# A fused attention and gated MLP kernel: w_in's DRAM writes queued behind batch 0's last store, w_out's blocks combined in batch 1's first half, seven products in its second

## The chip, the cores and the metric

The kernel runs on one core of a Trainium2 chip. The core has a matmul engine (TensorE, PE in the profile; its weight loads are shown as PEld), a vector engine (VectorE, DVE), a scalar engine (ScalarE, ACT), a general engine (GpSimd, POOL) and a queueing engine (SyncE, SP). Each works through its own instructions in order and meets the others at semaphores. On-chip data lies in SBUF, matmul results in the eight banks of PSUM, everything else in DRAM; 16 DMA engines move data between DRAM and SBUF. Nearly all DMAs of this kernel are issued by SP.

The metric is device time in microseconds of one execution, lower is better.

## The reference

The computation is a packed attention followed by a gated MLP. There are 8 batches with 8 heads, 576 positions and head dimension 64; 32 packed queries `p` per head first attend to the keys, then the 576 queries attend to the 32 results:

```python
p_packed = sm_attn(p, k, v)              # softmax(p k^T / 8) v, per batch and head
out = sm_attn(q, p_packed, p_packed)
x = out.transpose(0, 2, 1, 3).reshape(4608, 512)
h = x @ w_in                             # 512 x 2048
g = h * np.clip(h + 3.0, 0.0, 6.0) / 6.0
return g @ w_out                         # 2048 x 512
```

All inputs are float32 to the reference; `w_in` and `w_out` come as 64-bit words that the kernel narrows to float32 itself (lines 173 to 199).

## The kernel before

**The two products.** The kernel never forms `x`. For each batch it makes `m` = packed result times `w_in` (256 x 2048: 8 heads with 32 packed rows each; `u_m`, line 518, in four column chunks n) and multiplies the second softmax's weights by it. The 2048 columns of the hidden layer are walked in 16 blocks `f` of 128. For each block, `first_product` (line 912) makes the hidden values of up to 320 positions, `gate_into` (928) applies ACT's relu and DVE's min-and-multiply, `split` (935) makes a high part (ACT copy, rounded) and a low part (POOL subtraction), and the second product multiplies them by the rows of `w_out` that belong to `f`. Every exact product is three matmuls of rounded parts: high x high, high x low, low x high. So the first product of a block is 2 groups of 3 matmuls, and the second is 3 matmuls for each 128 positions, 512 columns wide.

**Halves of a batch.** A batch's 576 positions are done in two halves c = 0 and 1. One of them is "wide": it also computes 64 edge positions, kept in `bnd` and multiplied with those of a neighbouring batch, 128 at a time (`edge_parts`, `edge_product`). Second products wait in the list `pend` and are issued one or two blocks late, so that the matmul engine has other work while the gate is made.

**The seven products.** `moe_pairs` (1071) takes the blocks f = 0 to 7 as four pairs. A pair is a 2 x 2 matrix of 128-wide blocks times the 2 x 2 blocks of `w_out` (B11, B12 in the rows of block 2i; B21, B22 in those of 2i + 1; each 128 x 256). Instead of eight block products it makes seven, from sums of the blocks: S1 to S4 of the gated values (four additions on DVE, lines 1171 to 1174) and T1 to T4 of `w_out`. Each product is 3 matmuls, 256 columns wide. They are gathered in four PSUM banks A to D, whose numbers stand in `roles`. The blocks 8 to 15 are done singly. Batches 2 to 7 use `moe_pairs`; batch 1 uses `moe` (997), which does all 16 blocks singly; batch 0 has code of its own, `first_moe` (1202).

**combine.** The T blocks are made once, during batch 1, by `combine(i)` (1040), i = 0 to 3. T1, T2 and T4 go to new tiles that take the room of w_in's chunks 1 to 3 in SBUF (`wt`, tags `w_in1` to `w_in3`); T3 overwrites B12 inside `w_out`. Each `combine` adds high and low part of the two rows of blocks on POOL, makes the differences on DVE, then the parts on ACT and DVE. It is a generator: `fill` (1360), called ahead of each block f, moves it on by three steps in the second half from f = 2i + 4.

**w_in.** Later batches need w_in again, but only chunk 0's room (`w_in0`) stays for it. `keep_w_in(n)` (1334) writes the narrowed chunk n, 1 MB, to the DRAM tile `w_kept`; `fetch_w_in(n)` (1337) reads it back for the `u_m` of the next batch. Before the change `fill` calls `keep_w_in` in the first four blocks of batch 1.

**What sets the order.** Batch 0 follows `PLAN` (31 to 51), an order written by hand for all five engines; `lo` and `li` in it are loads of weights, `o0` to `o3` batch 0's output stores (`stored`, 1248). From batch 1 on, the order of the instructions on each engine is worked out ahead, when the program is built, from dependences and priorities; `issue_after(x)` keeps what is traced inside it behind x on x's engine. Nothing keeps `keep_w_in` behind batch 0's instructions, so its DMAs stand among batch 0's loads on SP. `fill` also brings in the next batch's attention: `inputs` (loads and transposes) from step 0, `packed` (the first softmax and its product) from step 6, `ahead` (`u_s2`, the second softmax) from step 19 of batch 1's 32 steps (`STAGES`, 23).

**PSUM.** `moe` takes its banks in turn from four (`next_acc`): three in the wide half, then two. The scores of the next batch's attention take a bank that is free; once `roles` is set, `u_s2` makes its scores in two rounds instead of one (478).

Of the kernel before, what the change touches and what calls it, by code (L numbers as in the profile page):

```python
# [10 lines left out]
F32 = mybir.dt.float32  # L11
# [5 lines left out]
ALU = mybir.AluOpType  # L17
# [7 lines left out]

LATE = (3, 2, 1, 2, 1)
PAIRS = 4

# [41 lines left out]
def packed_attention_moe(  # L72
# [17 lines left out]
    nc = tc.nc  # L90
    B, H, S, D = q.shape
    NPK = p.shape[2]
    DM, DF = w_in.shape
# [32 lines left out]
    def wo_at(part, f):  # L126
        return wo[f >= EARLY][part][:, f - EARLY * (f >= EARLY)]
# [912 lines left out]
    def combine(i):  # L1040

        if i == 0:
            for n in (2, 3, 1):
                for k in range(4):
                    blocks[len(blocks)] = n, k
            tiles = {
                n: wr.tile([P, 4, 2, H2], F32R, name=f"wt{n}", tag=f"w_in{n}") for n in (1, 2, 3)
            }
            for k in range(3 * PAIRS):
                n, at = blocks.pop(k)  # L1050
                blocks[k // 3, ("T1", "T2", "T4")[k % 3]] = [tiles[n][:, at, x] for x in range(2)]
        x = [xp.tile([P, 6 * P], F32, name="wx", tag="raw") for _ in range(2)]
        for k in range(2):
            hi, lo = (wo_at(part, 2 * i + k).bitcast(F32) for part in ("hi", "lo"))
            nc.gpsimd.tensor_tensor(out=x[k][:, :DM], in0=hi, in1=lo, op=ALU.add)
            yield
        b11, b12, t1 = (x[0][:, k * H2:(k + 1) * H2] for k in range(3))
        b21, b22, t2 = (x[1][:, k * H2:(k + 1) * H2] for k in range(3))
        nc.vector.tensor_sub(out=t1, in0=b12, in1=b11)
        nc.vector.tensor_sub(out=t2, in0=b22, in1=t1)  # L1060
        yield
        nc.vector.tensor_sub(out=b12, in0=b12, in1=b22)
        nc.vector.tensor_sub(out=b21, in0=b21, in1=t2)
        yield
        for name, made in (("T1", t1), ("T2", t2), ("T4", b21), ("T3", b12)):
            hi, lo = block(i, name)
            nc.scalar.copy(out=hi, in_=made)
            nc.vector.tensor_sub(out=lo, in0=made, in1=hi.bitcast(F32))
            yield

    def moe_pairs(b, c, fill):

# [129 lines left out]
    def first_moe(chains):  # L1202
# [45 lines left out]
        def stored(i):  # L1248

            osb = gp.tile([P, DM], F32, name="osb")  # L1250
            nc.scalar.activation(out=osb, in_=accs[i], func=AF.Copy, scale=1.0 / 6.0)
            yield
            rows = out[:4 * P].rearrange("(r c) m -> c r m", c=4)[2 * (i % 2) + i // 2]
            nc.sync.dma_start(out=rows, in_=osb)
            yield

        for f in range(NF):
# [91 lines left out]
    for b in range(1, B):  # L1349
# [10 lines left out]
        def fill(c, f):  # L1360
            s = c * NF + f
            with behind_gates():
                if b == 1:
                    for _ in range(LATE[s] if s < len(LATE) else 0):
                        next(late, None)
                    if s < NCH:
                        keep_w_in(s)
                    for i in range(PAIRS):
                        if c and f >= 2 * i + 4:
                            for _ in range(3):  # L1370
                                next(turned[i], None)
                else:
                    if s > 0:
                        next(late, None)
# [8 lines left out]
                        next(chain, None)  # L1383

        for c in range(2):
            if b == 1:
                moe(b, (c,), lambda f, c=c: fill(c, f))
            else:
                moe_pairs(b, c, lambda f, c=c: fill(c, f))
        if b == 1:  # L1390
            rest(*turned)
            roles.extend((acc_count[0] + i) % 4 for i in (2, 3, 0, 1))
    with tc.manual_schedule(engines={mybir.EngineType.PE}):
        second(0)

# [28 lines left out]
```

## Time and profile before

| | us |
|---|---|
| median of 3 runs | 727.02 |
| lowest, highest | 725.9, 727.23 |
| the profiled execution | 728.73 |
| its span on the core | 727.0 |

The profile is of one execution. Its span runs from the first to the last instruction on the core; the profiled execution's own time also has what lies around it. A second table shows how the span is used in 40 equal slices (18.2 us each): each digit is the busy share in tenths, PEclk is the clock granted to the matmul engine in tenths of full speed, DMA the mean share of the 16 DMA engines.

```profile
PE   6598899999989999999999999999999999999997
DVE  2896678541898568674596567685396856964252
PEclk9799999999999999999999999999999999999999
DMA  9999973435117162543524445272342723320000
```

The first six slices are batch 0, in most of which the DMA engines are at nine tenths or more. Batch 1's first half begins in slice 7 (counted from one), its second half about slice 10, batch 2 in slice 13. Other parts of the profile used below are the timelines of single engines (start, duration, engine, line, operation, output and inputs, and in brackets the idle time before it and what ended it), groups of instructions by line (busy us, mean ns of one, idle time before) and the chain of waits (start, duration, engine, output, line). The matmul engine's durations overlap, since its matmuls are pipelined; the chain's pieces do not.

### The profile page before, as it was taken

Reading aid. Unit: us, or ns where it says so; the run is one execution under the profiler, and the core shown is the slowest. Engines: PE = TensorE matmul, PEld = TensorE weight load, DVE = VectorE, ACT = ScalarE, POOL = GpSimd, SP = SyncE. Lnnn points to the kernel's source line nnn. Section 1 sums busy time; section 2 is a strip of 40 time slices with the busy share of each in tenths; the row PEclk is TensorE's granted clock in tenths of the full one; section 3 lists DMA queues with packets and bytes.
Section 4 is the critical chain, followed back from the end, with each engine's and each line's share of the span. In section 5 each row is a group of like instructions: output and inputs, shape, how many; then the busy total and the mean of one; then the engine's idle time right before and its main releaser. Section 6 shows DMA issues by size and latency. Waiting matters only on the chain.

```text
span 727.0 us, 15138 instructions
## 1 busy us (share of the span) xinstructions
PE 696.1 (96%) x5636; PEld 584.1 (80%) x5636; DVE 466.7 (64%) x1021; ACT 404.1 (56%) x884; POOL 354.2 (49%) x503
## 2 busy tenths in 40 slices
PE   6598899999989999999999999999999999999997
PEld 4476777788758887898887988798887988789896
DVE  2896678541898568674596567685396856964252
ACT  5797776553556555565355555555365554654362
POOL 2564440434455455474263535566353535557462
PEclk9799999999999999999999999999999999999999
DMA  9999973435117162543524445272342723320000
GB/s 280 294 259 265 262 226 85 85 61 125 73 58 175 30 154 79 167 78 62 139 71 156 79 96 149 74 175 50 91 119 81 166 54 98 116 87 1 27 19 29
DMA packets 195066, 85.41 MB, mean 117 GB/s; under 512 B 172976, under 2 KB 184752, under 8 KB 191408
## 3 DMA queue, kind: packets, MB, share of 16 engines
q1 hardware_dynamic: 194448, 84.24, 44.4%
q8 instruction: 44, 0.72, 0.4%
q14 instruction: 30, 0.25, 0.1%
q10 hardware_dynamic: 544, 0.20, 0.1%
HBM read 70.78 MB, written 13.63 MB: 116 GB/s over the span
## 4 chain that ended last, share of the span: by engine, by line
PE 79%; DVE 9%; DMA 5%; ACT 2%; SPq 2%; issue 2%; POOL 1%; ACTq 0%; POOLq 0%; DVEq 0%
PE acc L952 46%; PE ps_hh L919 23%; PE ps L340 5%; PE ps_h L597 2%; PE ps L460 1%; DMA room<-in_q_dram 1%; DMA w_again<-w_kept 1%; DVE t L931 1%; DMA out_dram<-osb_j 1%; PE ps L430 1%; SPq L284 1%; DMA raw_out<-in_moe_w_out_dram 1%; DMA raw_in<-in_moe_w_in_dram 1%; DVE z L505 1%; DMA p_nat<-in_p_dram 1%
## 5 line engine op out<-in xcount | busy, mean ns | idle before, releaser
L952 PE MATMUL acc<-wo_hi,g 128*128 128x512 f32 x512 | 182.6, 399 | 2.9 <-POOL g L937 2.9
L931 DVE SCALAR_TENSOR_TENSOR t<-t,ps_hh 128x320 f32<-128x320 f32 (+1 forms) x176 | 79.1, 449 | 121.3 <-ACT t L930 114.5
L937 POOL TENSOR_TENSOR g<-t,g 128x256 fp32r<-128x256 f32 x128 | 101.5, 794 | 86.2 <-ACT g L936 69.2
L919 PE MATMUL ps_hh<-a_hi,m_hi 128*128 128x320 f32 (+1 forms) x448 | 136.0, 304 | 1.9 <-DVE t L931 1.8
L930 ACT ACTIVATE t<-ps_hh,three 128x320 f32<-128x320 f32 (+1 forms) x176 | 88.0, 500 | 83.5 <-PE ps_hh L919 75.4
L919 PE MATMUL ps_hh<-a_hi,m_lo 128*128 128x320 f32 (+1 forms) x448 | 133.1, 297 | 0.0
L919 PE MATMUL ps_hh<-a_lo,m_hi 128*128 128x320 f32 (+1 forms) x448 | 132.8, 297 | 0.0
L952 PEld LDWEIGHTS acc<-wo_hi,g 128*128 128x128 f32 x512 | 94.8, 188 | 30.4 <-POOL g L937 6.5
L919 PEld LDWEIGHTS ps_hh<-a_hi,m_hi 128*128 128x128 f32 x448 | 84.7, 189 | 20.8 <-DVE t L931 5.6
L952 PE MATMUL acc<-wo_lo,g 128*128 128x512 f32 x256 | 100.9, 394 | 0.0
L919 PEld LDWEIGHTS ps_hh<-a_lo,m_hi 128*128 128x128 f32 x448 | 84.8, 189 | 6.0 <-issue 1.4
L937 POOL TENSOR_TENSOR ga<-tb,ga 128x256 fp32r<-128x256 f32 x96 | 59.9, 625 | 57.8 <-ACT ga L936 52.0
L919 PEld LDWEIGHTS ps_hh<-a_hi,m_lo 128*128 128x128 f32 x448 | 84.8, 189 | 3.9 <-issue 3.4
L936 ACT CAST g<-t 128x256 fp32r<-128x256 f32 x128 | 51.8, 405 | 49.8 <-DVE t L931 48.8
L937 POOL TENSOR_TENSOR gl<-t,gh 128x512 fp32r<-128x512 f32 x48 | 64.1, 1335 | 18.6 <-DMA out_dram<-osb_j 6.3
L948 POOL COPY bnd<-t 128x64 f32<-128x64 f32 x88 | 23.6, 269 | 94.8 <-DVE t L931 92.3
L545 DVE STREAM_TRANSPOSE tr<-nat 128x576 f32<-128x576 f32 x56 | 42.3, 766 | 25.1 <-DMA nat<-in_q_dram 14.3
L952 PE MATMUL acc<-wo_hi,gl 128*128 128x256 f32 (+1 forms) x160 | 52.5, 328 | 2.3 <-DVE gl L1230 1.3
L952 PE MATMUL acc<-wo_hi,gh 128*128 128x256 f32 (+1 forms) x160 | 54.0, 337 | 0.0
L952 PEld LDWEIGHTS acc<-wo_lo,g 128*128 128x128 f32 x256 | 48.3, 189 | 6.9 <-issue 0.8
L952 PE MATMUL acc<-wo_hi,ga 128*128 128x256 f32 x192 | 53.1, 283 | 0.0
L952 PE MATMUL acc<-wo_lo,gh 128*128 128x256 f32 (+1 forms) x160 | 52.1, 326 | 0.0
(213 smaller groups left out, 1503.7 us busy)
## 6 DMA issues: line engine op xcount, KB each, us to landing
w_again<-w_kept SPq DMA_DIRECT2D x24, 1024.0 KB, 4.9
out_dram<-osb SPq DMA_DIRECT2D x33, 256.0 KB, 2.5
nat<-in_k_dram SPq DMA_DIRECT2D x112, 72.0 KB, 2.8
nat<-in_q_dram SPq DMA_DIRECT2D x112, 72.0 KB, 2.6
raw_out<-in_moe_w_out_dram SPq DMA_DIRECT2D x10, 512.0 KB, 5.0
raw_in<-in_moe_w_in_dram SPq DMA_DIRECT2D x10, 512.0 KB, 5.8
w_kept<-w_in_sb SPq DMA_DIRECT2D x4, 1024.0 KB, 6.9
v_nat<-in_v_dram SPq DMA_DIRECT2D x28, 128.0 KB, 2.9
```

The source lines that it names most:

```text
L284: nc.sync.dma_start(out=t[r:r + 32], in_=src[b, 2 * a + h, :, 32 * c:32 * c + 32].rearrange("(t i) j -> i t j", i=32),)
L340: nc.tensor.matmul(pair[x][NPK * a:NPK * a + NPK, :n], rows[half, a], c, start=True, stop=True)
L430: nc.tensor.transpose(out=pair[x][:, c * P:(c + 1) * P], in_=e[x][:, c * P:(c + 1) * P], identity=ident)
L545: nc.vector.transpose(out=t, in_=state.pop(("nat", which, b, a)))
L597: nc.tensor.matmul(h[:, hf, :HS], mm[:, g, fs], aa[:, hf * HS:(hf + 1) * HS], start=(g == 0 and i == 0), stop=(g == NG - 1 and i == 2),)
L919: state["first"] = nc.tensor.matmul(h[:, :n], mm[:, g, fs], aa[:, t0:t0 + n], start=(g == 0 and i == 0), stop=(g == NG - 1 and i == 2),)
L930: state["relu"] = nc.scalar.activation(out=t[:, :n], in_=h, func=AF.Relu, bias=three)
L931: state["gate"] = nc.vector.scalar_tensor_tensor(out=t[:, :n], in0=t[:, :n], scalar=6.0, in1=h, op0=ALU.min, op1=ALU.mult)
L936: nc.scalar.copy(out=hi, in_=x)
L937: nc.gpsimd.tensor_sub(out=lo, in0=x, in1=hi.bitcast(F32))
L948: nc.gpsimd.tensor_copy(out=bnd[:, f, side * REM:side * REM + REM], in_=t[:, boff:boff + REM])
L952: nc.tensor.matmul(out, lhs[x], rhs[y], start=first and i == 0, stop=last and i == 2, skip_group_check=True)
```

## The change

Three things are changed. First, `stored` keeps the last store of batch 0 in `state["stored"]`, and all four `keep_w_in` are traced in step 0 of batch 1 behind that store on SP's queue. Second, `combine` is written anew: it works with two tiles of 256 columns, which take the room of `tb` (a tile of the pairs) instead of `raw`, adds high and low part of B12 and B22 only, and takes B11 and B21 part by part in additional DVE instructions; its steps are spread over steps 5 to 15 of batch 1, the first half, by the table `TURN` (step numbers of `combine(0)` to `combine(3)`). The T tiles fill chunk 1's room first. Third, batch 1's second half is done by `moe_pairs`, and `roles` is set ahead of it.

```diff
@@ -25,6 +25,7 @@
 
 LATE = (3, 2, 1, 2, 1)
 PAIRS = 4
+TURN = ((5, 5, 6, 6, 7, 7, 7), (7, 8, 8, 9, 9, 9, 10), (10, 10, 11, 11, 12, 12, 12), (13, 13, 13, 14, 14, 15, 15))
 
 
 
@@ -1040,7 +1041,7 @@
     def combine(i):
 
         if i == 0:
-            for n in (2, 3, 1):
+            for n in (1, 2, 3):
                 for k in range(4):
                     blocks[len(blocks)] = n, k
             tiles = {
@@ -1049,24 +1050,39 @@
             for k in range(3 * PAIRS):
                 n, at = blocks.pop(k)
                 blocks[k // 3, ("T1", "T2", "T4")[k % 3]] = [tiles[n][:, at, x] for x in range(2)]
-        x = [xp.tile([P, 6 * P], F32, name="wx", tag="raw") for _ in range(2)]
-        for k in range(2):
-            hi, lo = (wo_at(part, 2 * i + k).bitcast(F32) for part in ("hi", "lo"))
-            nc.gpsimd.tensor_tensor(out=x[k][:, :DM], in0=hi, in1=lo, op=ALU.add)
-            yield
-        b11, b12, t1 = (x[0][:, k * H2:(k + 1) * H2] for k in range(3))
-        b21, b22, t2 = (x[1][:, k * H2:(k + 1) * H2] for k in range(3))
-        nc.vector.tensor_sub(out=t1, in0=b12, in1=b11)
-        nc.vector.tensor_sub(out=t2, in0=b22, in1=t1)
-        yield
-        nc.vector.tensor_sub(out=b12, in0=b12, in1=b22)
-        nc.vector.tensor_sub(out=b21, in0=b21, in1=t2)
-        yield
-        for name, made in (("T1", t1), ("T2", t2), ("T4", b21), ("T3", b12)):
+        x, y = (xp.tile([P, W + P], F32, name="wx", tag="tb")[:, :H2] for _ in range(2))
+
+        def whole(dst, name):
+            hi, lo = (z.bitcast(F32) for z in block(i, name))
+            nc.gpsimd.tensor_tensor(out=dst, in0=hi, in1=lo, op=ALU.add)
+
+        def parted(name, made):
             hi, lo = block(i, name)
             nc.scalar.copy(out=hi, in_=made)
             nc.vector.tensor_sub(out=lo, in0=made, in1=hi.bitcast(F32))
-            yield
+
+        whole(x, "T3")
+        yield
+        whole(y, "B22")
+        yield
+        nc.vector.tensor_sub(out=y, in0=x, in1=y)
+        hi, lo = (z.bitcast(F32) for z in block(i, "B11"))
+        nc.vector.tensor_sub(out=x, in0=x, in1=hi)
+        nc.vector.tensor_sub(out=x, in0=x, in1=lo)
+        yield
+        parted("T1", x)
+        yield
+        nc.vector.tensor_sub(out=x, in0=hi, in1=y)
+        nc.vector.tensor_add(out=x, in0=x, in1=lo)
+        parted("T2", x)
+        yield
+        hi, lo = (z.bitcast(F32) for z in block(i, "B21"))
+        nc.vector.tensor_sub(out=x, in0=hi, in1=x)
+        nc.vector.tensor_add(out=x, in0=x, in1=lo)
+        parted("T4", x)
+        yield
+        parted("T3", y)
+        yield
 
     def moe_pairs(b, c, fill):
 
@@ -1251,7 +1267,7 @@
             nc.scalar.activation(out=osb, in_=accs[i], func=AF.Copy, scale=1.0 / 6.0)
             yield
             rows = out[:4 * P].rearrange("(r c) m -> c r m", c=4)[2 * (i % 2) + i // 2]
-            nc.sync.dma_start(out=rows, in_=osb)
+            state["stored"] = nc.sync.dma_start(out=rows, in_=osb)
             yield
 
         for f in range(NF):
@@ -1363,12 +1379,13 @@
                 if b == 1:
                     for _ in range(LATE[s] if s < len(LATE) else 0):
                         next(late, None)
-                    if s < NCH:
-                        keep_w_in(s)
+                    if s == 0:
+                        with tc.issue_after(state["stored"].ins):
+                            for n in range(NCH):
+                                keep_w_in(n)
                     for i in range(PAIRS):
-                        if c and f >= 2 * i + 4:
-                            for _ in range(3):
-                                next(turned[i], None)
+                        for _ in range(TURN[i].count(s)):
+                            next(turned[i], None)
                 else:
                     if s > 0:
                         next(late, None)
@@ -1383,13 +1400,12 @@
                         next(chain, None)
 
         for c in range(2):
-            if b == 1:
+            if (b, c) == (1, 0):
                 moe(b, (c,), lambda f, c=c: fill(c, f))
+                rest(*turned)
+                roles.extend((3, 0, 1, 2))
             else:
                 moe_pairs(b, c, lambda f, c=c: fill(c, f))
-        if b == 1:
-            rest(*turned)
-            roles.extend((acc_count[0] + i) % 4 for i in (2, 3, 0, 1))
     with tc.manual_schedule(engines={mybir.EngineType.PE}):
         second(0)
```

## The prediction

> **What bounds the kernel now.** First the page's busy shares, then the table by stretches.
>
> ```profile
> span 727.0 us, 15138 instructions
> PE 696.1 (96%) x5636; PEld 584.1 (80%) x5636; DVE 466.7 (64%) x1021; ACT 404.1 (56%) x884; POOL 354.2 (49%) x503
> ```
>
> PE is busy 96% of the span, so time is won only where PE stands, or where it has less to do. The starts of the first product's matmuls cut the span into halves of a batch. Batch 1's first half runs from 124.86 to 174.61, its second to 220.53; batch 3's second half, which already takes seven products, from 347.39 to 390.54. Columns: length, then busy time and instructions of PE, PEld, DVE, ACT, POOL; granted clock, DMA share, GB/s.
>
> ```profile
> 124.86:174.61 49.75, 49.75 (x378) 40.20 (x376) 20.25 (x46) 24.29 (x56) 20.75 (x40) 1.00 0.42 89
> 174.61:220.53 45.92, 41.71 (x278) 30.82 (x277) 36.21 (x72) 24.14 (x59) 24.73 (x24) 1.00 0.22 71
> 194.00:200.00 6.00, 5.15 (x28) 3.87 (x27) 6.00 (x14) 4.15 (x10) 3.79 (x4) 1.00 0.34 141
> 200.00:206.00 6.00, 4.43 (x23) 2.90 (x21) 6.00 (x11) 2.63 (x6) 3.04 (x4) 1.00 0.00 0
> 206.00:212.00 6.00, 5.88 (x44) 4.03 (x43) 6.00 (x13) 4.04 (x10) 3.02 (x4) 1.00 0.48 175
> 212.00:218.00 6.00, 4.33 (x22) 3.25 (x22) 5.05 (x9) 3.24 (x10) 4.22 (x4) 1.00 0.00 1
> 347.39:390.54 43.15, 42.64 (x406) 35.22 (x404) 30.44 (x64) 20.96 (x47) 18.29 (x23) 1.00 0.38 108
> 215.36 0.97 PE L952 MATMUL acc<-wo_hi,g 128*128 128x512 f32 x3 [1.60 <-POOL g L937]
> ```
>
> **Batch 1's second half is bound by DVE.** DVE is full from 194 to 212, and PE stands 0.85 + 1.57 + 0.12 + 1.67 = 4.2 us from 194 to 218. PE's timeline (last row) names POOL's low parts; POOL is not full there, but its inputs come through DVE's gate. This is where `combine` and batch 2's second softmax share DVE.
>
> **Batch 0 is bound by loads.** Rows of the timelines, in order of time; the bracket is the idle time before the row and what ended it.
>
> ```profile
> 41.04 0.39 SPq L1335 DMA_DIRECT2D w_kept<-w_in_sb  x1
> 52.59 0.55 SPq L1335 DMA_DIRECT2D w_kept<-w_in_sb  x1
> 53.23 7.56 SPq L284 DMA_DIRECT2D nat<-in_q_dram  x4
> 65.31 0.78 DVE L545 STREAM_TRANSPOSE tr<-nat 128x576 f32<-128x576 f32 x1 [3.12 <-DMA nat<-in_q_dram]
> 66.71 0.50 PE L952 MATMUL acc<-wo_hi,gl 128*128 128x512 f32 x1 [1.31 <-DVE gl L1230]
> 69.05 0.40 PE L597 MATMUL ps_h<-a_hi,m_hi 128*128 128x288 f32 x1 [0.45 <-DVE t L1223]
> 78.01 0.60 SPq L1335 DMA_DIRECT2D w_kept<-w_in_sb  x1
> 85.38 0.78 DVE L545 STREAM_TRANSPOSE tr<-nat 128x576 f32<-128x576 f32 x1 [2.54 <-DMA nat<-in_q_dram]
> 87.26 0.67 ACT L187 ACTIVATE raw_out<-raw_out 128x512 f32<-128x512 f32 x1 [2.66 <-DMA raw_out<-in_moe_w_out_dram]
> 89.39 0.40 PE L597 MATMUL ps_h<-a_hi,m_hi 128*128 128x288 f32 x1 [2.13 <-DVE t L1223]
> 86.00:92.00 6.00, 3.87 (x38) 2.98 (x41) 4.63 (x11) 4.49 (x8) 2.13 (x3) 0.90 1.00 280
> 92.00:98.00 6.00, 6.00 (x116) 4.25 (x106) 3.31 (x9) 4.61 (x8) 3.99 (x4) 0.82 0.82 281
> DMA to landing us min/median/max: 4.3/6.9/11.7
> ```
>
> Read it so: a 1 MB write of w_in goes out at 52.59; the queue's next four loads then take 7.56 us merely to issue; DVE stands 3.12 us for one of them, and PE follows (1.31 + 0.45). The same happens behind the write at 78.01: DVE 2.54, ACT 2.66, PE 2.13. Then the granted clock falls to 0.90 and 0.82 for two stretches of 6 us: 6 x 0.10 + 6 x 0.18 = 1.7 us of full clock. The last row gives the four writes' times to landing, 4.3 to 11.7 us.
>
> **Part 1: the writes leave batch 0.** Three of the four lie in the crowded stretch. What hangs on them is 1.31 + 0.45 + 2.13 = 3.9 us of standing and 1.7 us of clock, 5.6 together. The first write, at 41.04, goes too. All else is kept: the plan's order on PE, DVE, ACT, POOL and SP is fixed by hand, so the loads simply land earlier. I take 4.8: some 0.8 us for the next load that becomes the latest (from 86 to 92 DMA is 100% busy with loads alone). Bounds: 0, if the loads are late anyway, and 5.6; I stay near the top because both waits end directly behind a write.
>
> The Trainium skill (TensorE: Matmul & The Clock Gate, "What's actually happening") says the half-rate clock comes after at least one idle window of about 3.4 us. This trace shows the drop after 2.13 us of standing, so the trace decides; by the page the drop would have another cause and part 1 would be 1.7 us smaller.
>
> **Part 2: seven products in batch 1's second half.** Matmul pieces of the chain of waits, old form and batch 2's pair form; then DVE and POOL groups of this half (busy us, mean ns, idle before); the last row is line 505 in batch 3's second half.
>
> ```profile
> 177.61 2.80 PE acc L952 x12
> 228.03 1.44 PE acc L952 x12
> L1068 DVE TENSOR_TENSOR wt<-wx,wt 128x256 fp32r<-128x256 f32 x12 | 6.1, 517 | 0.5 <-ACT wt L1067 0.5
> L1059 DVE TENSOR_TENSOR wx<-wx 128x256 f32<-128x256 f32 x4 | 3.4, 860 | 0.5 <-POOL wx L1055 0.5
> L1060 DVE TENSOR_TENSOR wx<-wx 128x256 f32<-128x256 f32 x4 | 2.4, 607 | 0.1
> L1063 DVE TENSOR_TENSOR wx<-wx 128x256 f32<-128x256 f32 x4 | 1.9, 473 | 0.0
> L1062 DVE TENSOR_TENSOR wx<-wx 128x256 f32<-128x256 f32 x4 | 1.6, 412 | 0.0
> L1055 POOL TENSOR_TENSOR wx<-wo_hi,wo_lo 128x512 f32<-128x512 f32 x8 | 10.7, 1348 | 8.9 <-DVE wt L1068 4.2 <-ACT g L936 2.7 <-DVE wo_lo L1068 1.5
> L505 DVE TENSOR_TENSOR z<-z,den 128x576 f32<-128x576 f32 x2 | 2.6, 1305 | 0.0
> L505 DVE TENSOR_TENSOR z<-z,den 128x576 f32<-128x576 f32 x2 | 1.9, 934 | 0.0
> ```
>
> A 512-column matmul costs 2.80 / 12 = 0.233 us, a 256-column one 1.44 / 12 = 0.120. Eight blocks f of 6 wide ones (11.2 us) become four pairs of 21 narrow ones (84 x 0.120 = 10.1): 1.1 us less. The 32 DVE instructions of `combine` leave: 28 in the rows above (15.4 us) and four low parts of T3, about 17 with them, of the half's 36.2; the pairs bring 16 additions of 128 columns, at most half a row of 412 to 860 ns each, some 3 to 7 us. DVE then holds 22 to 26 us of about 41, so it is no longer full, and PE's 4.2 us should go. I take back 0.3, because batch 2's scores now come in two rounds and its softmax, two steps per block, falls beside the pairs. Part 2: -1.1 - 4.2 + 0.3 = **-5.0**, so 40.9 us. A check from another side: batch 3's second half, of the new shape, took 43.15 with another batch's attention in it too. Bounds: -2.8 (43.15) to -6.7 (all standing and unexplained gaps gone).
>
> **Part 3: combine in the first half.**
>
> ```profile
> 140.00:172.00 32.00, 32.00 (x266) 26.49 (x265) 10.51 (x27) 13.77 (x34) 12.83 (x24) 1.00 0.28 59
> ```
>
> It now has 4 x 11 = 44 DVE instructions of 256 columns (0.41 us each by the undisturbed row, 18.1 us), 16 copies on ACT (6.6, priced like DVE's) and 8 POOL additions of half the old width (8 x 1.348 / 2 = 5.4), which stand in POOL's queue ahead of the low parts that PE reads. They fall in blocks 5 to 15 of 49.75 / 16 = 3.1 us, so about 140 to 172 us, where DVE has 10.5 of 32 us: 28.6 after, ACT 20.4, POOL 18.2. This fits, beside matmuls that run two blocks ahead. If the cover fails, the price is what the full DVE costs today, 4.2. Bounds 0 to 4.2; I take **+0.8**.
>
> **Part 4: four writes behind the last store.** Chain, timeline and DMA rows.
>
> ```profile
> 128.49 4.12 SPq L284 DMA_DIRECT2D nat<-in_k_dram  x8
> 134.70 0.78 DVE L545 STREAM_TRANSPOSE tr<-nat 128x576 f32<-128x576 f32 x1 [0.74 <-DMA nat<-in_k_dram]
> 143.05 0.65 PE ps L340 x16
> w_again<-w_kept SPq DMA_DIRECT2D x24, 1024.0 KB, 4.9
> v_high<-in_v_dram SPq DMA_DIRECT2D x56, 64.0 KB, 2.2
> 122.93 3.98 SPq L1254 DMA_DIRECT2D out_dram<-osb  x4
> ```
>
> On SP the order becomes: batch 0's four stores (to 126.9), four writes (0.4 to 0.6 us of issue each, as above), then batch 2's third and fourth k block, its q blocks and v. V's tile takes w_in chunk 0's room and so waits for write 0; it is read only behind the scores, after 143. The T blocks wait for writes 1 to 3; the first falls in block 6, at 124.9 + 6 x 3.1 = 143.5. A transfer of 1 MB needs 4.9 - 2.2 = 2.7 us more than a small one (estimate from the last DMA rows), four 10.8. The k blocks, in DVE's hands at 134.70 today, come some 8 us later relative to the stores, near 143, just when their score matmuls start (143.05). DVE's order is fixed, so a transpose that stands there holds the gates, with two blocks (about 6 us) in hand. I take **+0.7**; bounds 0 and 9.
>
> **Part 5: seams.** The first pair needs bank 2, whose copy by ACT comes third and waits for a store's buffer: +0.2 (0 to 1). Batch 2's first half then follows pairs instead of `moe`, as batch 4's follows batch 3's: 0.
>
> **Sum:** -4.8 - 5.0 + 0.8 + 0.7 + 0.2 = -8.1. The profiled execution took 728.73 us, 1.7 of it around the span; it becomes 720.6. It lies 1.7 above the median of the runs shown, 727.02, from which the same step gives **718.9**.
>
> **Rivals.**
> A. The loads are late anyway (part 1 is worth 0). For it: DMA is 100% busy at 86 to 92, with no write in flight. Against it: both long waits end right behind a write. 723.7; chance 0.13.
> B. The first half's DVE becomes the bound (part 3 costs 4.2 or more): 28.6 of 32 us, with waits for ACT inside each block. Against: its blocks last 3.1 us, those of the new second half 40.9 / 16 = 2.6. 722.3; chance 0.14. The Trainium skill (SBUF — State Buffer, "Who interferes with whom") says a DVE instruction with two SBUF inputs and a GpSimd one that reads SBUF block each other wholly. The trace agrees: line 505 took 1305 ns beside `combine`'s POOL additions and 934 without them.
> C. The pairs' own DVE work fills the second half again, so that it takes 43.15 and more: 721.1 to 723.9; chance 0.06.
> D. **Slower:** the four writes hold the queue. At the crowded median of 6.9 us each instead of 2.7, the k blocks come 16.8 us later still; PE stands at batch 2's score matmuls (143.05 today). 727.0 - 9.8 + 1.0 + 16.8 = 735.0. It decides from about 4.9 us per write, where 4 x 2.2 = 8.8 eats the gain. Against it: DMA's share in this half is 0.42 today, and the quickest write landed in 4.3 us, the fixed part included. Chance 0.07.
> E. Half of A and half of B and D: no change. Chance 0.05.
>
> **How the numbers follow.** My case has 0.55; A, B and C are faster too: 0.88. Within 0.2% (1.45 us, about what a measurement of this kernel can tell from no change) 0.05, slower 0.07. The range goes from 714 (parts 1 and 2 near their ends, nothing lost) to 726, which holds A, B and C and leaves out D and E.
>
> **What would show it.** Right: no `w_kept` row ahead of the last store; no idle DVE before `tr<-nat` near 65 and 85; clock 1.00 at 86 to 98; batch 1's second half at 39 to 42 us; its first half within 2 us of 49.75 (124.86 to 174.61 by the same starts). Wrong: idle PE near 143 ended by scores or `nat`; DVE full in 140 to 172; PE still waiting for POOL's `g` in the second half.

## The result, and the profile after

| | before | after |
|---|---|---|
| median | 726.46 | 717.45 |
| lowest to highest (4 runs each) | 725.85 to 727.23 | 717.11 to 717.54 |
| the profiled execution | 728.73 | 717.11 |
| its span | 727.0 | 715.3 |

The ratio is 0.9875, with a 95% interval of 0.9858 to 0.9892. The medians differ by 9.0 us, the two profiled executions by 11.6: the execution of before that was profiled lay 2.3 above its median, that of after 0.3 below. Of the runs below, one execution of e9_both took 1120.71 us at a granted clock of 0.56, where its three others took 713.58 to 714.08, and that kernel's row leaves it out.

The page of the kernel after, busy time of each engine:

```profile
span 715.3 us, 15241 instructions
PE 694.2 (97%) x5672; PEld 586.1 (82%) x5672; DVE 478.0 (67%) x1054; ACT 404.6 (57%) x887; POOL 356.2 (50%) x508
```

PE has 1.9 us less busy time, DVE 11.3 more. So 9.7 of the 11.6 us by which the span is shorter are time in which PE stood.

The kernel after by stretches: two windows late in batch 0, the two halves of batch 1, and the blocks in which `combine` now runs (columns as before: length; busy time and count of PE, PEld, DVE, ACT, POOL; granted clock, DMA share, GB/s).

```profile
86.00:92.00 6.00, 6.00 (x131) 4.27 (x130) 3.77 (x11) 5.30 (x9) 3.90 (x3) 1.00 0.90 266
92.00:98.00 6.00, 6.00 (x41) 4.12 (x40) 5.82 (x12) 4.53 (x8) 3.22 (x4) 1.00 0.25 79
119.14:169.12 49.98, 49.83 (x377) 40.05 (x375) 37.72 (x80) 28.13 (x68) 26.18 (x43) 1.00 0.61 157
169.12:211.37 42.25, 40.43 (x317) 33.05 (x316) 31.16 (x70) 23.61 (x54) 19.66 (x24) 1.00 0.40 110
140.00:172.00 32.00, 31.85 (x266) 26.04 (x265) 27.30 (x59) 17.42 (x45) 17.83 (x29) 1.00 0.40 77
```

Batch 0 ends at 119.14 instead of 124.86. At 86 to 98 PE is busy all the time at full clock, where it stood and ran at 0.90 and 0.82 before. In batch 1's second half PE stands 42.25 - 40.43 = 1.8 us, where it stood 4.2. The first half holds 17.5 us more of DVE and is 0.2 longer.

Cut by the starts of the first product's matmuls, as in the prediction, the stages compare so (us; the stages that are not listed differ by 0.1 or less each):

| stage | before | after | difference |
|---|---|---|---|
| batch 0 | 124.86 | 119.14 | -5.72 |
| batch 1, first half | 49.75 | 49.98 | +0.23 |
| batch 1, second half | 45.92 | 42.25 | -3.67 |
| batch 2, first half | 36.24 | 35.69 | -0.55 |
| batch 4, first half | 36.97 | 35.69 | -1.28 |
| batch 5, second half | 43.13 | 42.61 | -0.52 |

The timelines of SP, DVE and PE of the kernel after, in order of time (start, duration, engine, line, operation, and in brackets the idle time before it and what ended it):

```profile
81.14 0.78 DVE L546 STREAM_TRANSPOSE tr<-nat 128x576 f32<-128x576 f32 x1 [0.18 <-DMA nat<-in_q_dram]
117.22 4.00 SPq L1270 DMA_DIRECT2D out_dram<-osb  x4
121.27 3.88 SPq L1351 DMA_DIRECT2D w_kept<-w_in_sb  x4
125.25 10.59 SPq L285 DMA_DIRECT2D nat<-in_k_dram  x8
136.51 0.78 DVE L546 STREAM_TRANSPOSE tr<-nat 128x576 f32<-128x576 f32 x1 [1.15 <-DMA nat<-in_k_dram]
173.90 0.33 PE L471 MATMUL ps_x<-ident,pn 128*128 128x128 f32 x1 [0.88 <-DVE pn L465]
193.71 0.39 PE L953 MATMUL acc<-wo_hi,gh 128*128 128x256 f32 x1 [0.62 <-ACT gh L937]
195.08 0.39 PE L953 MATMUL acc<-wo_hi,gl 128*128 128x256 f32 x1 [0.32 <-POOL gl L938]
```

The transposes of batch 0 hardly wait any more (0.18 us before the one at 81.14, against 2.54 before its counterpart). The four writes stand behind the four stores, and the eight small loads behind them take 10.59 us to issue, where they took 4.12. So batch 2's k comes later, and DVE stands 1.15 us for it at 136.51, but PE does not stand there. What is left of PE's waits in the second half is three: the longest, 0.88 us, is for `pn`, the normalized result of batch 2's first softmax (DVE, line 465).

### The profile page after: what moved, and what is told of

Read it like the earlier page. It is cut to its first block, busy times and chain, and to the rows that moved or that the text cites. A ratio compares the mean times of both kernels' runs of the same rounds, so it can differ in the third digit from the quotient of the medians.

```text
span 715.3 us, 15241 instructions
## 1 busy us (share of the span) xinstructions
PE 694.2 (97%) x5672; PEld 586.1 (82%) x5672; DVE 478.0 (67%) x1054; ACT 404.6 (57%) x887; POOL 356.2 (50%) x508
## 4 chain that ended last, share of the span: by engine, by line
PE 83%; DVE 11%; DMA 2%; ACT 2%; POOL 1%; issue 1%; SPq 0%; DVEq 0%; ACTq 0%; POOLq 0%
PE acc L953 48%; PE ps_hh L920 23%; PE ps L341 5%; PE ps_h L598 3%; PE ps L461 1%; PE ps L431 1%; DVE t L932 1%; PE ps_t L669 1%; DMA k_nat<-in_k_dram 1%; DVE wt L1062 1%; PE ps L264 1%; DVE z L495 1%; PE ps_w L711 0%; DVE den L500 0%; DVE den L502 0%
## 5 line engine op out<-in xcount | busy, mean ns | idle before, releaser
L953 PE MATMUL acc<-wo_hi,g 128*128 128x512 f32 x480 | 171.3, 399 | 0.0
L938 POOL TENSOR_TENSOR g<-t,g 128x256 fp32r<-128x256 f32 x120 | 94.0, 784 | 77.6 <-ACT g L937 65.1
L953 PEld LDWEIGHTS acc<-wo_hi,g 128*128 128x128 f32 x480 | 89.4, 189 | 24.7 <-POOL g L938 2.5
L938 POOL TENSOR_TENSOR ga<-tb,ga 128x256 fp32r<-128x256 f32 x104 | 66.8, 642 | 69.6 <-ACT ga L937 59.1
L953 PE MATMUL acc<-wo_lo,g 128*128 128x512 f32 x240 | 94.8, 395 | 0.0
L938 POOL TENSOR_TENSOR gl<-t,gh 128x512 fp32r<-128x512 f32 x52 | 69.2, 1331 | 20.8 <-ACT gh L937 7.5
L937 ACT CAST g<-t 128x256 fp32r<-128x256 f32 x120 | 48.5, 404 | 42.4 <-DVE t L932 41.4
L949 POOL COPY bnd<-t 128x64 f32<-128x64 f32 x88 | 24.5, 278 | 80.1 <-DVE t L932 78.3
L953 PE MATMUL acc<-wo_hi,ga 128*128 128x256 f32 x208 | 57.4, 284 | 0.0
L953 PE MATMUL acc<-wo_hi,gh 128*128 128x256 f32 (+1 forms) x168 | 56.3, 335 | 0.6 <-ACT gh L937 0.6
L953 PE MATMUL acc<-wo_hi,gl 128*128 128x256 f32 (+1 forms) x168 | 54.8, 326 | 0.8 <-POOL gl L938 0.8
L937 ACT CAST ga<-tb 128x256 fp32r<-128x256 f32 x104 | 36.5, 351 | 33.7 <-DVE tb L932 29.7
```

The costliest lines, as they stand in the source:

```text
L937: nc.scalar.copy(out=hi, in_=x)
L938: nc.gpsimd.tensor_sub(out=lo, in0=x, in1=hi.bitcast(F32))
L949: nc.gpsimd.tensor_copy(out=bnd[:, f, side * REM:side * REM + REM], in_=t[:, boff:boff + REM])
L953: nc.tensor.matmul(out, lhs[x], rhs[y], start=first and i == 0, stop=last and i == 2, skip_group_check=True)
```

## The experiments

Twelve runs follow: ten changed kernels, and both kernels once more. They came in three groups, and each group had its own runs of the kernel before. All stage lengths in this table are from profiles, cut as above; "halves" is both halves of batch 1.

| kernel | median | ratio to before (95%) | batch 0 | halves | 2, first half | 4, first half |
|---|---|---|---|---|---|---|
| before, profiled again | 729.98 (one run) | | 126.10 | 95.66 | 36.23 | 36.94 |
| e1_writes_only | 722.55 | 0.9926 (0.9898 to 0.9953) | 118.75 | 96.96 | 35.91 | 35.79 |
| e2_pairs_only | 720.79 | 0.9908 (0.9879 to 0.9938) | 122.53 | 91.03 | 35.77 | 35.69 |
| e3_no_pairs | 720.41 | 0.99 (0.9873 to 0.9928) | 119.20 | 91.84 | 36.74 | 38.25 |
| e4_turn_earlier | 718.52 | 0.9876 (0.9852 to 0.9899) | 119.06 | 93.54 | 35.69 | 35.69 |
| after_again | 717.93 | 0.988 (0.986 to 0.9901) | 119.03 | 92.73 | 35.69 | 35.69 |
| e5_writes_behind_k | 716.07 | 0.9857 (0.9836 to 0.9878) | 118.80 | 91.04 | 35.69 | 35.69 |
| e6_double_writes | 714.37 (one run) | | 118.07 | 90.37 | 35.87 | 35.69 |
| e7_roles | 717.94 | 0.9878 (0.9854 to 0.9901) | 119.32 | 93.82 | 35.69 | 35.69 |
| e8_attention_later | 715.92 | 0.9855 (0.9828 to 0.9881) | 118.52 | 90.63 | 35.69 | 35.69 |
| e9_both | 713.60 (three runs) | 0.9822 (0.979 to 0.9853) | 118.75 | 89.09 | 35.69 | 35.69 |
| e10_no_pairs | 723.01 (one run) | | 119.02 | 89.87 | 39.49 | 39.76 |

The medians of the kernel before were 728.3 in the first group (e1 to e4), 727.07 in the second (after_again to e7) and 727.45 in the third (e8 to e10, before again).

**The parts alone.** The first takes the kernel before and only moves the writes; the second takes the kernel after and leaves the writes where they were.

```diff
# e1_writes_only, against before
-            nc.sync.dma_start(out=rows, in_=osb)
+            state["stored"] = nc.sync.dma_start(out=rows, in_=osb)
...
-                    if s < NCH:
-                        keep_w_in(s)
+                    if s == 0:
+                        with tc.issue_after(state["stored"].ins):
+                            for n in range(NCH):
+                                keep_w_in(n)
# e2_pairs_only, against after: the last hunk the other way round
```

> Only the four writes of w_in are moved behind batch 0's last store; combine and moe stay as before. If the writes delayed batch 0's loads (my theory), batch 1 starts at 118 to 120 us instead of 124.86, the clock stays 1.00 from 80 to 98, batch 1's second half stays at 45 to 46.5 us, and the time is 720 to 722 us. If the loads are late anyway, or the writes only move their cost into batch 1's first half, that half grows to 54 us or more or batch 1 starts after 123, and the time is 725 us or more.

> The new combine in the first half and seven products in the second, but the writes of w_in stand in batch 0 as before. If the two parts of the change are independent, batch 1 starts at 124 to 126 us, its two halves take 91 to 93 us together (95.67 before, 92.23 with the whole change), and the time is 722.5 to 724.5 us. If the late k blocks behind the writes are what fills the first half in the changed kernel, that half is here under 49 us and the two under 91; if the second half's gain needs the earlier batch 0, the two stay above 94.

By stretches, e1 and then e2: the two halves of batch 1, for e1 with a window of batch 0 ahead of them.

```profile
86.00:92.00 6.00, 6.00 (x130) 4.19 (x129) 3.51 (x10) 5.18 (x9) 3.88 (x3) 1.00 0.84 253
...
118.75:168.38 49.63, 49.63 (x376) 40.29 (x375) 20.07 (x45) 24.34 (x56) 21.08 (x40) 1.00 0.62 159
168.38:215.71 47.33, 41.73 (x280) 31.34 (x279) 35.78 (x73) 24.12 (x60) 24.10 (x23) 1.00 0.33 97
```

```profile
122.53:172.29 49.76, 49.76 (x377) 40.37 (x376) 37.03 (x84) 28.20 (x68) 26.49 (x43) 1.00 0.39 85
172.29:213.56 41.27, 40.44 (x315) 33.12 (x314) 30.32 (x66) 23.19 (x53) 18.76 (x24) 1.00 0.29 84
```

Moving the writes alone ends batch 0 at 118.75, 6.1 us ahead of before, with PE full and the clock at 1.00: part 1 is real, and rival A falls. The second half of e1 is still the old one, and longer than the 45 to 46.5 us expected: `combine` is in it, PE stands 47.33 - 41.73 = 5.6 us. e2 shows the other part alone: halves of 91.03 instead of 95.67, with 17 us of DVE moved into the first half and the first half no longer than before. And e2's halves are shorter than those of after (92.23, and 92.73 when it ran again): the late writes cost batch 1 from 1.2 to 1.7 us. e1 shows the same price, 96.96 against 95.67.

**The seven products.** e3 does batch 1's second half singly, block by block, with the moved `combine` and the moved writes kept. What this kernel leaves out is B12: T3 stands in its place in `w_out`, and block by block the half multiplies with T3, so the output is not the reference's. `roles` is also set later, which puts batch 2's scores back to one round.

```diff
-            if (b, c) == (1, 0):
+            if b == 1:
                 moe(b, (c,), lambda f, c=c: fill(c, f))
-                rest(*turned)
-                roles.extend((3, 0, 1, 2))
+                if c == 0:
+                    rest(*turned)
             else:
                 moe_pairs(b, c, lambda f, c=c: fill(c, f))
+        if b == 1:
+            roles.extend((acc_count[0] + i) % 4 for i in (2, 3, 0, 1))
```

> The whole change without the seven products: batch 1's second half goes through moe, block by block (there it multiplies with T3 where B12 stood in w_out, which takes the same time). If the gain of the second half is DVE's (combine gone from it) and the fewer matmul columns bring only 1.1 us, the second half takes 42.5 to 44 us against 45.92 before and 42.25 with pairs, and the time is 717.5 to 719.5 us. If the seven products are what shortens it, the second half stays at 45 us or more and the time at 720 us or more.

```profile
169.46:211.04 41.58, 40.50 (x281) 31.60 (x280) 25.09 (x51) 21.47 (x49) 13.62 (x19) 1.00 0.39 112
```

Its halves took 91.84, no longer than the 92.23 of after, and in the second half (the row above) PE is busy 40.50 us, against 40.43 with the seven products. So the second half is shorter because `combine` has left it, and not because of fewer columns. Yet the kernel is not as fast as after, because batch 2's and batch 4's first halves took 36.74 and 38.25 instead of 35.69. e10, below, follows that up.

**combine two blocks earlier**, so that its last DVE instruction comes ahead of the second half:

```diff
-TURN = ((5, 5, 6, 6, 7, 7, 7), (7, 8, 8, 9, 9, 9, 10), (10, 10, 11, 11, 12, 12, 12), (13, 13, 13, 14, 14, 15, 15))
+TURN = ((3, 3, 4, 4, 5, 5, 5), (5, 6, 6, 7, 7, 7, 8), (8, 8, 9, 9, 10, 10, 10), (11, 11, 11, 12, 12, 13, 13))
```

> The changed kernel with every step of combine two blocks earlier (steps 3 to 13 instead of 5 to 15). If combine's overrun past the first half (its last DVE instruction at 173.9, the second half's first matmul at 169.12) delays the seam, combine ends before 171, PE no longer waits for pn at 173.9, the two halves of batch 1 take 90 to 91.3 us instead of 92.23, and the time is 715.5 to 716.7 us. If DVE is simply full in the first half wherever the steps stand, or the seam costs nothing, the halves stay at 92 to 93 us and the time at 717 to 718 us.

A miss. `combine` ended at 167.24 and the wait for `pn` went, but the halves grew to 93.54. One of the new waits is in ACT's timeline of e4: the third copy of batch 1's first half waits for a store to free its buffer, and PE's pairs wait for that copy.

```profile
180.79 0.60 ACT L910 ACTIVATE osb<-acc 128x512 f32<-128x512 f32 x1 [3.15 <-DMA out_dram<-osb]
```

**The writes behind k.** e5 sends the four writes behind batch 2's last k block, chunk 1 first, and e6 keeps them as in after and adds four more of 1 MB each, to a spare tile in DRAM.

```diff
# e5_writes_behind_k
-                nc.sync.dma_start(
+                state["block"] = nc.sync.dma_start(
...
-                    if s == 0:
-                        with tc.issue_after(state["stored"].ins):
-                            for n in range(NCH):
+                    if s == 3:
+                        with tc.issue_after(state["block"].ins):
+                            for n in (1, 2, 3, 0):
# e6_double_writes
                             for n in range(NCH):
                                 keep_w_in(n)
+                            for n in range(NCH):
+                                nc.sync.dma_start(out=w_twice[n], in_=w_in_sb[0].rearrange("p f a e -> p (f a e)"))
```

> The changed kernel again, to be compared with the others on the same chip: by the profile before, batch 1 starts at 118.7 to 119.5 us, its two halves take 91.8 to 92.8 us, and the time is 9 us, give or take 1.5, below the kernel before.

> The changed kernel with the four writes one step further back: behind batch 2's third and fourth k block instead of behind batch 0's last store, chunk 1 first. If the late k blocks cost the difference between 92.23 us (the two halves of batch 1 in the changed kernel) and 91.03 us (with early writes), the k blocks are turned within 11 us of batch 1's start instead of 17 to 20, the halves take 90.8 to 91.5 us and the time falls by about 1.2 us against the changed kernel. If they cost nothing, the halves stay at 92 to 92.5 us.

> The changed kernel with four more writes of 1 MB (chunk 0 again, to a spare DRAM tile) behind the four, so with twice the data in the queue; nothing reads them. By the price of 2.4 us per write (landings at 126.5, 129.0, 131.4, 134.2) the k blocks come 10 us later still. If writes that hold the queue are what could make the change slower (rival D), batch 1's first half grows by 3 to 9 us over 49.98; if the order on DVE and the two blocks in hand absorb it, it grows by less than 1.5.

SP's queue in e5, and then the halves of e6 by stretches:

```profile
122.43 4.13 SPq L285 DMA_DIRECT2D nat<-in_k_dram  x8
126.61 3.21 SPq L1351 DMA_DIRECT2D w_kept<-w_in_sb  x4
129.91 11.79 SPq L285 DMA_DIRECT2D nat<-in_q_dram  x8
```

```profile
118.07:165.14 47.07, 47.07 (x287) 38.21 (x286) 34.88 (x69) 25.98 (x62) 26.94 (x43) 1.00 0.72 234
165.14:208.44 43.30, 42.45 (x406) 34.99 (x404) 33.03 (x81) 25.82 (x60) 18.39 (x24) 1.00 0.50 132
```

In e5 the eight k loads issue in 4.13 us again, and it is now the q loads that crawl (11.79 us), and PE does not stand for them. The halves are 91.04, as in e2 with its early writes: the price of the late writes is the delay of k, and it can be had back. e6 was to make that delay dear, if a longer queue costs time. k came 29.6 us after batch 1's start, some 12 us later than in after, and the kernel was no slower in its one run: 714.37, with halves of 90.37 (the first has fewer of the matmuls, 287 against 377, and the second more). So a long queue does not decide, which is against rival D. What made it faster is not isolated. Batch 2's first softmax moved back (its scores came 35.5 us after the start, against 23.5 in after), but most of it still shared DVE with `combine`, which ran from 14.5 to 55.4 us after the start. Only its end came clear of it: `pn` was made 61.4 us after the start, and in after at 54.2, between two of `combine`'s last instructions.

**The order of the banks.** e7 begins the pairs with another bank, `roles.extend((1, 2, 3, 0))`.

> The changed kernel with the four banks of the pairs in another order: C takes the bank that the first half leaves free and D the one that is copied out first, so that no bank of the first products is the third to be copied. If the seam's wait for the third copy matters, the second half shrinks by 0.3 to 1 us from 42.25; if the wait for pn (1.03 us) hides it, as I believe, it stays within 0.3 of it.

717.94, the time of after: a miss, since the second half neither shrank nor kept its length. The halves were 93.82, with PE waiting 1.41 us for `pn` in that profile.

**The attention later.** e8 is after with the first softmax of batch 2 begun in step 9 instead of 6; e9 is e5 with the same edit.

```diff
-STAGES = (((0, 1), (6, 2), (19, 2)), ((0, 1), (10, 2), (19, 1)))
+STAGES = (((0, 1), (9, 2), (19, 2)), ((0, 1), (10, 2), (19, 1)))
```

> The changed kernel with batch 2's first attention part (scores, exponentials, its product with v) from step 9 on instead of step 6; nothing else. If the first half is crowded because combine and this attention share DVE there, as the run with doubled writes suggests (it pushed the attention back and took 90.37 us), the two halves of batch 1 take 90.3 to 91.3 us against 92.23, pn is made within 2 us of the product with v, and the time falls by 0.8 to 2 us. If doubled writes helped in another way, the halves stay at 92 to 93 us.

> The writes behind batch 2's k blocks and the attention from step 9 on, together. If both cure the same crowd on DVE they don't add: the halves take 90.2 to 91.1 us (91.04 with the writes moved alone) and the time is 714.5 to 716.5 us. If they were separate gains they would add up to 89.5 us or less.

By stretches, the halves of e8, then those of e9:

```profile
118.52:168.41 49.89, 49.87 (x376) 40.15 (x375) 37.17 (x80) 27.79 (x67) 26.44 (x43) 1.00 0.61 157
168.41:209.15 40.74, 40.12 (x316) 32.88 (x315) 30.88 (x70) 23.45 (x54) 19.04 (x24) 1.00 0.40 114
```

```profile
118.75:168.39 49.64, 49.64 (x376) 40.28 (x375) 38.32 (x83) 29.17 (x70) 28.60 (x46) 1.00 0.60 158
168.39:207.84 39.45, 39.45 (x316) 32.84 (x315) 28.85 (x67) 22.64 (x51) 17.53 (x22) 1.00 0.41 118
```

e8's halves came out as expected, though in detail not for the reason given: `pn` still came 5.0 us behind its product. But PE's order has the matmul that reads `pn` 12 first-product matmuls later than in after (57.9 us after batch 1's start, not 54.8), and PE does not stand for it. The two gains add up: 92.23 in after, 91.04 with e5's edit, 90.63 with e8's, 89.09 with both, and in both halves of e9 PE is busy the whole time. e9 is the fastest of all by repeated runs, faster than both kernels.

**The seven products again, without the crowd.** e10 is e5 with e3's edit, so it too multiplies with T3 where B12 stood.

> The writes behind batch 2's k blocks, and batch 1's second half through moe, without the seven products (there T3 stands where B12 stood in w_out). If the seven products are worth their 1.1 us of matmul columns where DVE is less crowded, batch 1's halves and batch 2's first half take 127.8 us or more together, against 91.04 + 35.69 = 126.73 with them. If DVE's additions for the pairs eat it, the sum is within 0.6 of 126.73.

Without the seven products the halves are even 1.2 us shorter (89.87 against 91.04), but batch 2's and batch 4's first halves are 3.8 and 4.1 longer. Here are e10's second half of batch 1, PE's timeline of e10 at the first of these places, a window behind it, and the DMA view of the stretch from 208.2 to 216.3 (a queue's packets, MB and share of the 16 engines; an issue's size and us to landing):

```profile
168.78:208.89 40.11, 40.11 (x279) 31.67 (x278) 22.96 (x47) 21.14 (x48) 13.79 (x19) 1.00 0.31 86
```

```profile
216.38 1.96 PE L341 MATMUL ps<-w_again,pps 64*32 64x512 f32 x16 [2.37 <-DMA w_again<-w_kept]
```

```profile
216.00:218.00 2.00, 1.62 (x16) 0.26 (x16) 0.74 (x2) 0.00 (x0) 0.33 (x1) 0.52 0.81 268
```

```profile
q8 instruction: 1, 0.02, 1.0%
...
w_again<-w_kept SPq DMA_DIRECT2D x1, 1024.0 KB, 7.8
```

PE stands for chunk 3 of w_in, the last of the four that `fetch_w_in` brings back (`w_again`), and then runs at half clock. In e5 the same fetch is issued just as far ahead of its use (PE is free for it about 5.5 us after its issue in both), but lands in 5.0 us instead of 7.8. The kernel before was profiled a second time to see whether its long first half of batch 4 comes with the kernel.

> The kernel before, profiled once more, to see what of its stages repeats: batch 1 starts at 122.5 to 125.5 us, its halves take 95 to 97.5 us, and batch 4's first half takes 35.7 us if the 36.97 of the first profile was one late fetch of w_in, 37 if it belongs to the kernel.

It does: 36.97 and then 36.94. It is the same wait as e10's, and after has none there. PE's timeline of before at that place, its DMA view (389.9 to 396.8), and then that of after (380 to 385.3):

```profile
396.86 1.09 PE L340 MATMUL ps<-w_again,pps 64*32 64x512 f32 x16 [1.21 <-DMA w_again<-w_kept]
```

```profile
q8 instruction: 1, 0.02, 1.0%
...
w_again<-w_kept SPq DMA_DIRECT2D x1, 1024.0 KB, 6.6
```

```profile
q1 hardware_dynamic: 883, 1.14, 69.7%
w_again<-w_kept SPq DMA_DIRECT2D x1, 1024.0 KB, 4.9
```

The slow fetches have a transfer of 16 KB beside them, on a queue that the profile calls instruction, presumably a piece of the program being loaded; the quick one has none. Over batch 2's fetches of chunk 3 in all fourteen profiles: five have such a transfer begin within 0.9 us of their issue (before in both its profiles, e1, e3, e10) and took 5.21 to 7.75 us; nine have none and took 4.79 to 5.49, so the two ranges overlap a little. The five are just the profiles in which batch 1 does no seven products; a program of another length would load its pieces at other moments. In e10's packets most of the fetch is done by 213.0, and a few of its 8 KB pieces, one behind the other, end at 215.4, as one late DMA engine would leave them. In batch 4 such a transfer begins within 0.3 us of this fetch in before (both profiles), e3 and e10, which took 6.56 to 7.87; the ten other profiles have none there and took 4.78 to 5.10. A neighbour of this kind is not enough by itself: after's fetch of chunk 1 for batch 2, at 187.49, has one and took 4.83. Nor does every slow fetch have one at its issue: e3's, at 189.57, has none and took 6.38. That a load of the program makes the fetch late is read from the profiles; no run moved the load alone, so it is not shown.

## Why the prediction was right, and where its sizes were off

The time forecast, 718.9, was 1.5 above the median measured, and the mechanism held. By terms the agreement is less close than that: the sum took 8.1 off a profiled execution of 728.73, and the profiled one of after is 11.6 lower.

**Part 1, -4.8: right, measured -5.7** (-6.1 in e1). Both waits went, with the clock's drop behind them, and next to nothing took their place; the 0.8 us kept back for "the next load that becomes the latest" was not needed. The term is less exact than either figure, because batch 0 with early writes ended at 122.53, 124.86 and 126.10 in three profiles, and with late ones within 118.07 to 119.32 in eleven. Any difference from 3.2 to 8.0 could have been read from one pair; that the forecast lies within 1.5 us of the measured median is in part luck.

The clock's drop counted for 1.7 us there, in doubt by the Trainium skill (TensorE: Matmul & The Clock Gate, "What's actually happening"), which puts half clock behind an idle window of some 3.4 us. The length of a wait by itself does not tell when it comes: PE stood 2.13 us in before and 2.37 and 2.49 in e10, and the clock dropped; it stood longer than 2.5 us in both other profiles with early writes, and the clock stayed. Here are PE's rows in before profiled again and in e2:

```profile
92.09 0.40 PE L597 MATMUL ps_h<-a_hi,m_hi 128*128 128x288 f32 x1 [2.85 <-DVE t L1223]
```

```profile
88.32 0.40 PE L598 MATMUL ps_h<-a_hi,m_hi 128*128 128x288 f32 x1 [2.52 <-DVE t L1239]
```

What does tell is where the wait falls. In every profile each stretch at half clock before the last microseconds lasts 3.41 us or a multiple of it, and the stretches of one profile begin a whole number of 3.41 us apart (in e10 at 216.09 and 390.17, 51 of them). Counted from these, the time falls into pieces of 3.41 us. Here are two neighbouring pieces each of before, of before profiled again and of e2, around the wait:

```profile
87.34:90.75 3.41, 1.36 (x10) 1.36 (x11) 2.56 (x6) 3.21 (x6) 1.72 (x2) 1.00 0.98 271
90.75:94.16 3.41, 3.41 (x85) 2.79 (x84) 1.03 (x4) 2.61 (x5) 2.50 (x2) 0.50 0.97 293
```

```profile
90.31:93.72 3.41, 1.63 (x12) 1.62 (x12) 2.78 (x6) 2.94 (x6) 1.68 (x2) 1.00 0.97 277
93.72:97.13 3.41, 3.41 (x97) 2.41 (x103) 1.82 (x6) 2.61 (x6) 2.47 (x2) 1.00 0.77 256
```

```profile
87.04:90.45 3.41, 2.13 (x36) 1.97 (x40) 2.76 (x6) 3.00 (x6) 0.96 (x2) 1.00 0.92 273
90.45:93.86 3.41, 3.41 (x103) 2.38 (x99) 1.66 (x6) 2.42 (x5) 2.57 (x2) 1.00 0.80 246
```

PE stood 3.41 - 1.36 = 2.05 us in the piece ahead of the drop in before, and 2.09 and 2.49 in those ahead of e10's two. The two longer waits lie across a border: no piece holds more than 1.78 us of the one and 1.28 of the other, and no drop follows. The window that the Trainium skill names has the length of these pieces; the traces show besides that PE need not stand through the whole of one. So the 1.7 us (half of 3.41) hang on where the wait falls as well as on its length, and may be there in one execution and not in the next.

**Part 2, -5.0: its larger piece right, its smaller one wrong.** The second half was to take 40.9 and took 42.25, which leaves rival C's 43.15 out. DVE is no longer full there, but it is not as free as forecast: it held 31.16 us of the half, not 22 to 26, since the pairs brought more than 3 to 7 us (e5's half has 30.71, e10's without them 22.96) and `combine` ran 5.2 us into it. "Eight blocks of 6 wide ones become four pairs of 21 narrow ones: 1.1 us less" did not show in the half: e3 without the seven products had halves 0.4 shorter than after, e10 1.2 shorter than e5. It did not show in PE's own busy time either, with 40.43 and 40.50 in after and e3, 40.45 and 40.11 in e5 and e10. Only in e9, where PE never stands, is the half shorter than e10's, 39.45 against 40.11, and these two differ in the start of the attention as well. That waits for the pairs' own additions and copies eat the saving is likely, and not shown.

**Part 3, +0.8: the size nearly right, the price of DVE's instructions wrong.** The first half grew by 0.23, and DVE's 27.30 us in 140 to 172 stand against the 28.6 expected. But that is because `combine` did not end there: its last DVE instruction ended at 174.35, 5.2 us into the second half. Its 44 instructions took 24.5 us, not 18.1. Two of its groups in after (busy us, mean ns of one, idle time before):

```profile
L1080 DVE TENSOR_TENSOR wx<-wo_hi,wx 128x256 f32<-128x256 f32 x4 | 3.1, 785 | 0.1
...
L1068 DVE TENSOR_TENSOR wx<-wx 128x256 f32<-128x256 f32 x4 | 1.7, 424 | 0.8 <-POOL wx L1057 0.8
```

The same operation on the same shape takes 424 ns on one line and 785 on another. The timelines of POOL and DVE show when:

```profile
145.08 0.79 POOL L938 TENSOR_TENSOR g<-t,g 128x256 fp32r<-128x256 f32 x1
148.70 0.37 POOL L949 COPY bnd<-t 128x64 f32<-128x64 f32 x1 [2.83 <-DVE t L932]
```

```profile
145.31 0.85 DVE L1070 TENSOR_TENSOR wx<-wx,wo_hi 128x256 f32<-128x256 f32 x1
146.19 0.42 DVE L1071 TENSOR_TENSOR wx<-wx,wo_lo 128x256 f32<-128x256 f32 x1
...
156.04 0.42 DVE L1070 TENSOR_TENSOR wx<-wx,wo_hi 128x256 f32<-128x256 f32 x1
```

Line 1070 takes 0.85 us while POOL makes a low part; line 1071 behind it takes 0.42 while POOL stands (for 2.83 us, up to 148.70), and so does line 1070 at 156.04, begun while POOL stood. The page that rival B cited for this, the Trainium skill's SBUF — State Buffer ("Who interferes with whom"), was borne out, and its rule belonged in the price of part 3: 412 ns was a row without a neighbour on POOL. The late end of `combine` is what `pn` queued behind on DVE, the 0.88 us wait at 173.90. So rival B was half there: DVE got near its bound, but PE paid in the second half.

**Part 4, +0.7: right in kind, a little small, 1.2 to 1.7.** k came 9.5 us later, where some 8 were expected. But PE did not stand at batch 2's score matmuls, since the order worked out when the program is built had put these later too, behind 54 first-product matmuls instead of 42. The price came through DVE: the delayed attention met `combine` there. That is also why rival D could not happen: the four writes landed 2.4 to 2.8 us behind one another, not 6.9, and even eight of them, in e6's one run, cost nothing.

**Part 5, +0.2 and 0.** The bank's wait did not show in after, nor in e2, e5, e8 and e9, where PE does not stand for `pn` either; it showed in e4 as 0.72 us, and another order of the banks brought nothing (e7). Batch 2's first half was forecast as unchanged and gained 0.55. That is no wait saved: PE did not stand there in before, and 0.47 of it are two wide matmuls that now run ahead of the border, in batch 1's second half. Batch 4's gained 1.28, nearly all of it the 1.21 us wait for chunk 3. It is not the seven products by themselves that took this wait away, since e1 does without them and has 35.79 there. These 1.8 us, 0.9 more in part 1, and 0.5 in batch 5's second half make up most of the 3.5 by which the terms fell short. Why batch 5's second half took 42.61 in after and 43.14 in e9 was not tried and stays open.

## What to carry to other kernels

When a load that is waited for stands right behind a large write that nobody waits for, move the write behind the loads of the next stage, and not merely out of this one: the same four writes cost 5.7 us ahead of batch 0's loads (3.2 to 8.0, by which two profiles are compared), 1.2 to 1.7 ahead of batch 2's k, and nothing behind it. When work is moved off a full engine, price it at its new place with the neighbours that it has there, and ask which small instruction of another chain will queue behind it; moving that chain by three steps was worth as much as moving the writes again. A saving in matmul columns is a forecast for the matmul engine's own time: look for it there, and do not count it in a stage where that engine still waits for others.

## What the runs showed of the hardware

- Batch 0 ended between 122.53 and 126.10 us in three profiles with early writes, and between 118.07 and 119.32 in eleven with late ones. The 30 runs of before in the groups spread from 724.84 to 730.64, the 8 of after from 717.11 to 718.46; but the numbers of runs differ, and e4 and e8, with late writes, spread by 2.6 and 3.0 us, so that the writes widen the spread of whole runs is not shown.
- The granted clock fell to half in pieces of 3.41 us that lie on one grid through a whole profile. From 40 us on it fell behind pieces in which PE stood 2.05 us or more (before, e10), and not behind those with 1.78 or less (before profiled again, e2, e3).
- A fetch of 1 MB that lands in 4.8 to 5.5 us took up to 7.75 in batch 2 and 7.87 in batch 4 in profiles where a 16 KB transfer on an instruction queue began beside its issue. If the one makes the other, a change of the instruction count moves time in stages that it does not touch.
- More traffic did not make the kernel slower (e6: four extra megabytes, 714.37 in one run against 717.93), since PE did not stand for what came later.
